# W_in's conversion issued behind P times V of its step instead of ahead of it

## The chip, the cores and the metric

The kernel runs on one core of one Trainium2 chip. The time is that of one execution in device microseconds; a kernel's time is the median of its runs. Engines are called TensorE (PE in the profile, PEld for its weight loads), VectorE (DVE), ScalarE (ACT), GpSimd (POOL) and SyncE (SP, which here only issues DMAs).

## The reference, cut to what matters

```python
scores = q @ k^T / 8                      # 4 batches x 12 heads, 448 x 448, head size 64
p = exp(30 * tanh(scores / 30))           # kept as numerators, divided by their sums later
x = (p / p.sum(-1)) @ v                   # laid out as 1792 x 768
x = soft_moe(x, phi, w1, w2)              # 8 experts, 32 slots in all
out = (prelu(x @ w_in, alpha)) @ w_out    # w_in 768 x 2048, w_out 2048 x 768, both float64
```

The last two weights arrive as float64 (two 32-bit words to a number) and are turned to float32 on the chip.

## The kernel before, in words

**Stages.** Attention takes the 48 heads as 24 pairs. Then come the eight experts (`experts`, weights w1 and w2 streamed from DRAM), and then the network of W_in and W_out (`mlp`).

**The loop around the change.** Attention is one loop over steps g. A pair has four steps, one for each chunk of keys, in the order 0, 3, 1, 2 (chunk 3 holds the tail of 64 keys of both heads). Step g does, in the order of the source: the scores of its chunk and on ScalarE their tanh (line 381) and exp (line 382), both into the tile `p` (`qk`); at a pair's second step the transposes of the next pair's k and q, with a copy `kh` on ScalarE (line 346) and three operations on VectorE (`kl`, `qh`, `ql`); work put off from earlier steps (`run_bg`: row sums, reciprocals, norms, logits, slot sums); loads of k and q two pairs ahead; the store of a W_in piece that was converted two steps before (`store_w_in`, line 680, which also loads the next raw piece, line 660); the conversion of a W_in piece (`conv_w_in`); at some steps a prefetch of expert weights (line 157); and P times V for the chunk of two steps before (`pv`). At steps g = 4i + 1 that chunk is its pair's last: there ScalarE copies the pair's numerators of x from the PSUM tile `o` to `xu` (line 406). `o` has one buffer, so the first P times V of the next pair, one step later, waits for this copy. GpSimd adds the `p` tiles up for the row sums (lines 397, 401, 404).

**The conversion.** W_in has 24 pieces of 128 x 512. Each goes through `to_f32`: one absolute value on ScalarE (line 178), then four operations on VectorE (lines 179, 183, 186, 189), all on the tile `cvbuf`. The steps are 4, 7, 10, 13, 16, 19, 22, 25, 29 and from there every fourth, to 89; 18 of the 24 are thus steps of the `xu` copy. The store of the last piece frees the place of `cvbuf` for expert weights.

**What sets the order.** Each engine runs its instructions in an order fixed at compile time. A planner works through the source order with a clock of its own: an instruction that is not ready by that clock is passed by a later one of its engine that is. `to_f32` ties its absolute value behind the last matmul issued so far (`order[0]`) and its first VectorE operation behind the last `ql` (`latest[0]`); these ties carry no wait on the chip, they only hold the planner. SyncE's queue issues DMAs in its order, and one that waits holds up those behind it.

Of the kernel before, what the change touches and what calls it, by code (L numbers as in the profile page):

```python
# [24 lines left out]
def tile_attention_soft_moe_mlp(ctx, tc, q, k, v, cap, phi, w1, w2, w_in, w_out, alpha, out):  # L25
# [90 lines left out]
    def load_early(after):  # L116

        key = loads[NA]
        where[key] = [load_quarter(*key, c, t, after) for c, t in enumerate(early)]
# [56 lines left out]
    def to_f32(raw, t, after=()):  # L176
        lo, hi = raw[..., 0], raw[..., 1]
        first = nc.scalar.activation(out=t, in_=hi.bitcast(F32), func=AF.Abs, scale=65536.0)
        then = nc.vector.tensor_scalar(out=t, in0=t, scalar1=H_MIN, scalar2=H_MAX, op0=ALU.max, op1=ALU.min)
        for ins, before in zip((first, then), after):  # L180
            tc.add_manual_dep(ins.ins, before.ins.name, NOSYNC, reason="not before its step")
        tu = t.bitcast(U32)
        nc.vector.tensor_scalar(
            out=tu, in0=tu, scalar1=4, scalar2=1, op0=ALU.logical_shift_left, op1=ALU.logical_shift_right
        )
        nc.vector.scalar_tensor_tensor(
            out=tu, in0=lo, scalar=29, in1=tu, op0=ALU.logical_shift_right, op1=ALU.bitwise_or
        )
        nc.vector.scalar_tensor_tensor(
            out=tu, in0=hi, scalar=0x80000000, in1=tu, op0=ALU.bitwise_and, op1=ALU.bitwise_or  # L190
        )
# [35 lines left out]
    def attention():  # L227
        with ExitStack() as pools:
# [69 lines left out]
            def tails(nm, i, src):  # L298
                if nm == "k":
                    for u in range(2):  # L300
                        nc.sync.dma_start(out=ktails[i % 2][head(u), u, :], in_=src[u, KEYS:, :])
                    return
                for u in range(2):
                    nc.sync.dma_start(out=nat["v", i][head(u), 2 * JK, :], in_=src[u, KEYS:, :])

            def load(i, names):
                if i >= NPAIR:
                    return None
                b, m = divmod(i, NP)
                for nm in names:  # L310
                    src = {"k": k, "q": q, "v": v}[nm][b, 2 * m:2 * m + 2]

                    if nm == "q":
                        t = nat_p[i % 2].tile([P, J, 2, D], F32, tag=nm, name=nm)
                        for h in range(2):
                            ins = nc.sync.dma_start(
                                out=t[:, :, h, :], in_=src[h].rearrange("(p j) d -> p j d", j=J)
                            )
                    elif nm == "k":
                        t = nat_p[i % 2].tile([128, 2 * JK, D], F32, tag=nm, name=nm)  # L320
                        by_j = t[:, :2 * JK, :].rearrange("p (j h) d -> p j h d", h=2)
                        for h in range(2):
                            ins = nc.sync.dma_start(
                                out=by_j[:, :, h, :], in_=src[h, :KEYS, :].rearrange("(p j) d -> p j d", j=JK)
                            )
                    else:
                        t = v_p[i % 2].tile([128, 2 * JK + 1, D], F32, tag=nm, name=nm)
                        ins = nc.sync.dma_start(
                            out=t[:, :2 * JK, :].rearrange("p (h j) d -> p h j d", h=2),
                            in_=src[:, :KEYS, :].rearrange("h (p j) d -> p h j d", j=JK),  # L330
                        )
                    nat[nm, i] = t
                    if nm != "q" and (i or nm == "v"):
                        tails(nm, i, src)
                return ins

            def trans_k(i):

                t = nat["k", i].rearrange("p (j h) d -> p j (h d)", h=2)
                ps = aux([128, KEYS + 2 * TAIL], "tr")  # L340
                for j in range(JK):
                    transpose(ps[:, 128 * j:128 * j + 128], t[:, j], ident)
                transpose(ps[:, KEYS:], ktails[i % 2].rearrange("p h d -> p (h d)"), ident)
                kh = stk_p[i % 2].tile([128, KEYS + 2 * TAIL], F32R, tag="kh", name="kh")
                kl = stk_p[i % 2].tile([128, KEYS + 2 * TAIL], F32R, tag="kl", name="kl")
                nc.scalar.activation(out=kh, in_=ps, func=AF.Copy)
                nc.vector.tensor_sub(out=kl, in0=ps, in1=kh)
                stk["k", i] = (kh, kl)
# [17 lines left out]
            def qk(i, c):  # L366

                kh, kl = stk["k", i]
                qh, ql = stk["q", i]
                ps = ps_s.tile([128, 2, 512], F32, tag="s", name="s")  # L370
                for n, (a, b) in enumerate(((kh, qh), (kh, ql), (kl, qh))):
                    flags = dict(start=(n == 0), stop=(n == 2))
                    if c == JK:
                        matmul(ps[:, 0, :S], a[:, KEYS:], b, **flags)
                        continue
                    for u in range(2):
                        o = 128 * c
                        matmul(ps[:, u, :S], a[head(u), o:o + 128], b[head(u)], **flags)
                n = 1 if c == JK else 2
                pe = (ptt_p if c == JK else pt_p).tile([128, n, S], F32, tag="p", name="p")  # L380
                nc.scalar.activation(out=pe, in_=ps[:, :n, :S], func=AF.Tanh)  # L381
                nc.scalar.activation(out=pe, in_=pe, func=AF.Exp, scale=cap_sb)  # L382
                pt[i, c] = pe
# [271 lines left out]
            def load_w_in(i):  # L655
                if i >= ncv:
                    return
                fb, kk = divmod(i, KD)
                craw[i] = cvbuf[:, i % 2].rearrange("p (f t) -> p f t", t=2)
                nc.sync.dma_start(out=craw[i], in_=w_in[kk * 128:(kk + 1) * 128, fb * 512:(fb + 1) * 512, :])  # L660

            ncv = KD * (DFF // 512)
# [6 lines left out]
            def cv_at(n):  # L669
                return cv_steps[n]  # L670

            def conv_w_in(i):
                fb, kk = divmod(i, KD)
                t = cvbuf[:, 2, i % 2 * 512:i % 2 * 512 + 512].bitcast(F32)
                to_f32(craw.pop(i), t, (order[0], latest[0]))
                cout[i] = t
# [8 lines left out]
            def run_bg():  # L685
                while bg and min(bg) <= now[0]:
                    for fn, a in bg.pop(min(bg)):
                        fn(*a)
# [18 lines left out]
            for g in range(NPAIR * J + LAG):  # L707
                now[0] = g
                i, c = divmod(g, J)
                if g == 14:  # L710
                    nc.sync.dma_start(out=alpha_sb, in_=alpha.rearrange("(k p) -> p k", p=128))
                if g == 17:
                    nc.vector.tensor_scalar(out=nalpha_sb, in0=alpha_sb, scalar1=-1.0, scalar2=None, op0=ALU.mult)
                if i < NPAIR:
                    qk(i, CHUNKS[c])
                    if c == 1 and i + 1 < NPAIR:
                        trans_k(i + 1)
                        trans_q(i + 1)
                run_bg()
                if i < NPAIR:  # L720
                    if c == 0:
                        last = load(i + 2, "kq") or last
                    if c == 2:
                        if i == NPAIR - LAG - 1:
                            load_early(last)
                    if g == 2:
                        load_w_in(0)
                        load_w_in(1)
                    for n in range(ncv):
                        if cv_at(n) == g - 2:  # L730
                            store_w_in(n)
                        if cv_at(n) == g:
                            conv_w_in(n)
                    if c == 3 and i in LOADS and may_load() is not None:
                        load_next(last)
                if g >= LAG:
                    n, e = divmod(g - LAG, J)
                    pv(n, CHUNKS[e])
                    if e == J - 1:
                        load(n + 2, "v")  # L740
            order.clear()
            while bg:
                now[0] += 1
# [18 lines left out]
    def tail():  # L762
# [254 lines left out]
        with (  # L1017
# [3 lines left out]
            with tc.tile_pool(name="ex2", bufs=1, reuse_waits="tile", side="right") as ex2_p:  # L1021
# [6 lines left out]
                with (  # L1028
# [9 lines left out]
                    mlp(ps_w, ps_c, ex_p, cv_p, g_p, ob_p, so, cstk)  # L1038

    attention()  # L1040
    tail()

# [29 lines left out]
```

## Time and profile before

| | us |
|---|---|
| median of 3 runs (618.27 to 625.05) | 618.63 |
| profiled execution | 618.59 |
| its span, first to last instruction | 616.20 |
| TensorE busy in the span | 574.9 |
| VectorE busy | 403.6 |
| ScalarE busy | 318.8 |
| GpSimd busy | 162.4 |

The span is one execution; 2.39 us of it lie around the span. Attention fills about the first 276 us, the experts run to about 345 us, the rest is the last network. Busy shares are means over these stages.

### The profile page before, as it was taken

Reading aid. Unit: us, or ns where it says so; the run is one execution under the profiler, and the core shown is the slowest. Engines: PE = TensorE matmul, PEld = TensorE weight load, DVE = VectorE, ACT = ScalarE, POOL = GpSimd, SP = SyncE. Lnnn points to the kernel's source line nnn. Section 1 sums busy time; section 2 is a strip of 40 time slices with the busy share of each in tenths; the row PEclk is TensorE's granted clock in tenths of the full one; section 3 lists DMA queues with packets and bytes.
Section 4 is the critical chain, followed back from the end, with each engine's and each line's share of the span. In section 5 each row is a group of like instructions: output and inputs, shape, how many; then the busy total and the mean of one; then the engine's idle time right before and its main releaser. Section 6 shows DMA issues by size and latency. Waiting matters only on the chain.

```text
span 616.2 us, 10737 instructions
## 1 busy us (share of the span) xinstructions
PE 574.9 (93%) x4110; PEld 386.6 (63%) x4110; DVE 403.6 (65%) x734; ACT 318.8 (52%) x509; POOL 162.4 (26%) x111
## 2 busy tenths in 40 slices
PE   6789889999999999989999899999999999999997
PEld 4344344445444444455455568888888888888886
DVE  4499896697669969551013499999566555555662
ACT  4788788788988778620011366764312121121211
POOL 0667586747574745500000000000000000000000
PEclk9899999999999999988999999999999999999999
DMA  4778877798887781799999999100301010010101
GB/s 104 196 219 214 262 233 242 194 254 234 249 246 212 200 246 48 252 376 373 405 403 406 388 406 391 78 1 1 104 1 51 1 31 22 0 52 2 51 1 51
DMA packets 95169, 110.90 MB, mean 180 GB/s; under 512 B 56208, under 2 KB 70032, under 8 KB 95120
## 3 DMA queue, kind: packets, MB, share of 16 engines
q1 hardware_dynamic: 94976, 110.24, 55.5%
q8 instruction: 32, 0.52, 0.4%
q14 instruction: 17, 0.14, 0.1%
q10 hardware_dynamic: 144, 0.00, 0.0%
HBM read 98.41 MB, written 11.80 MB: 179 GB/s over the span
## 4 chain that ended last, share of the span: by engine, by line
PE 64%; DVE 11%; DMA 10%; ACT 7%; POOL 4%; issue 2%; SPq 1%; ACTq 0%; POOLq 0%
PE oc L946 13%; PE oc L952 13%; PE oc L953 13%; DMA w<-in_moe_w_dram 7%; PE o L279 5%; PE s L279 5%; PE hps L901 2%; ACT p L382 2%; POOL acc L401 2%; PE aps L875 2%; POOL acc L397 2%; ACT p L381 2%; DMA k<-in_k_dram 2%; PE h L815 2%; PE tr L279 1%
## 5 line engine op out<-in xcount | busy, mean ns | idle before, releaser
L952 PE MATMUL oc<-wsp,gh 128*128 128x512 f32 x448 | 151.7, 339 | 0.0
L946 PE MATMUL oc<-wsp,gh 128*128 128x512 f32 x448 | 151.6, 338 | 0.0
L953 PE MATMUL oc<-wsp,gl 128*128 128x512 f32 x448 | 150.7, 337 | 0.0
L917 ACT ACTIVATE gh<-gf 128x256 fp32r<-128x256 f32 (+1 forms) x96 | 43.5, 453 | 132.9 <-DVE gf L916 126.9
L279 PE MATMUL o<-p,v 128*64 128x448 f32 (+1 forms) x384 | 94.0, 568 | 13.1 <-ACT xu L406 13.0
L381 ACT ACTIVATE p<-s 128x896 f32<-128x896 f32 x96 | 78.9, 823 | 29.6 <-PE s L279 18.8
L382 ACT ACTIVATE p<-p,cap 128x896 f32<-128x896 f32 x96 | 91.1, 950 | 2.3
L946 PEld LDWEIGHTS oc<-wsp,gh 128*128 128x128 f32 x448 | 85.0, 190 | 10.7 <-issue 0.9
L953 PEld LDWEIGHTS oc<-wsp,gl 128*128 128x128 f32 x448 | 84.7, 189 | 11.0 <-issue 1.2
L952 PEld LDWEIGHTS oc<-wsp,gh 128*128 128x128 f32 x448 | 85.0, 190 | 9.8 <-issue 0.4
L918 DVE TENSOR_TENSOR gl<-gf,gh 128x256 fp32r<-128x256 f32 (+1 forms) x96 | 45.0, 469 | 45.3 <-ACT gh L917 45.2
L397 POOL TENSOR_TENSOR acc<-p 128x896 f32<-128x896 f32 x24 | 53.6, 2235 | 79.2 <-ACT p L382 79.2
L279 PEld LDWEIGHTS s<-qh,kh 64*128 64x128 f32 (+1 forms) x168 | 17.9, 183 | 66.8 <-issue 27.8
L401 POOL TENSOR_TENSOR acc<-acc,p 64x448 f32<-64x448 f32 x46 | 55.2, 1201 | 3.2
L913 DVE TENSOR_SCALAR mn<-hps,alpha 128x256 f32<-128x256 f32 (+1 forms) x81 | 39.5, 487 | 23.5 <-PE hps L901 23.4
L404 POOL TENSOR_TENSOR acc<-acc,p 128x896 f32<-128x896 f32 x23 | 49.7, 2162 | 1.8
L279 PE MATMUL s<-qh,kh 64*128 64x448 f32 (+1 forms) x168 | 45.3, 469 | 0.0
L279 PEld LDWEIGHTS o<-p,v 128*64 128x64 f32 (+1 forms) x384 | 19.0, 134 | 38.1 <-ACT xu L406 19.3
L916 DVE SCALAR_TENSOR_TENSOR gf<-hps,mn 128x256 f32<-128x256 f32 (+1 forms) x81 | 34.6, 428 | 2.7
L279 PE MATMUL s<-qh,kl 64*128 64x448 f32 (+1 forms) x168 | 35.3, 364 | 0.0
L279 PE MATMUL s<-ql,kh 64*128 64x448 f32 (+1 forms) x168 | 35.1, 363 | 0.0
L837 PE MATMUL y<-w,hT 128*32 128x256 f32 x384 | 30.7, 382 | 1.8 <-DVE hT L830 1.1
(151 smaller groups left out, 780.9 us busy)
## 6 DMA issues: line engine op xcount, KB each, us to landing
w<-in_moe_w_dram SPq DMA_DIRECT2D x80, 384.0 KB, 7.9
w<-in_moe_w_dram SPq DMA_DIRECT2D x36, 512.0 KB, 8.1
cvbuf<-in_moe_w_in_dram SPq DMA_DIRECT2D x24, 512.0 KB, 4.9
w<-in_moe_w_out_dram SPq DMA_DIRECT2D x16, 768.0 KB, 9.0
w_in<-cvbuf SPq DMA_DIRECT2D x24, 256.0 KB, 2.5
q<-in_q_dram SPq DMA_DIRECT2D x48, 112.0 KB, 4.2
k<-in_k_dram SPq DMA_DIRECT2D x48, 96.0 KB, 5.0
v<-in_v_dram SPq DMA_DIRECT2D x24, 192.0 KB, 3.3
```

What stands on the lines that cost most here:

```text
L279: ins = nc.tensor.matmul(*a, **kw)
L381: nc.scalar.activation(out=pe, in_=ps[:, :n, :S], func=AF.Tanh)
L382: nc.scalar.activation(out=pe, in_=pe, func=AF.Exp, scale=cap_sb)
L397: nc.gpsimd.tensor_add(out=a, in0=pt[i, 0], in1=pe)
L401: nc.gpsimd.tensor_add(out=a[r, u, :], in0=a[r, u, :], in1=pt[i, JK][r, 0, :])
L404: nc.gpsimd.tensor_add(out=a, in0=a, in1=pe)
L913: nc.vector.tensor_scalar(out=mn, in0=ps, scalar1=0.0, scalar2=alpha_sb[:, f:f + 1], op0=ALU.min, op1=ALU.mult)
L917: nc.scalar.activation(out=gh, in_=gf, func=AF.Copy)
L918: nc.vector.tensor_sub(out=gl, in0=gf, in1=gh)
L946: ins = nc.tensor.matmul(o, gh[:, ts], wo_h[f][:, cols], start=(f == 0 and not second), stop=False)
L952: nc.tensor.matmul(o, gh[:, ts], wo_l[f][:, cols], start=False, stop=False)
L953: nc.tensor.matmul(o, gl[:, ts], wo_h[f][:, cols], start=False, stop=(f == KF - 1 and not more))
```

## The change

The two lines that issue a step's conversion move from ahead of `pv` to behind it. Everything else in the source stays, and the tie of the absolute value is now to the last matmul of `pv`, since that is the last one issued.

```diff
                     for n in range(ncv):
                         if cv_at(n) == g - 2:
                             store_w_in(n)
-                        if cv_at(n) == g:
-                            conv_w_in(n)
                     if c == 3 and i in LOADS and may_load() is not None:
                         load_next(last)
                 if g >= LAG:
                     n, e = divmod(g - LAG, J)
                     pv(n, CHUNKS[e])
                     if e == J - 1:
                         load(n + 2, "v")
+
+                for n in range(ncv):
+                    if cv_at(n) == g:
+                        conv_w_in(n)
```

## Rows read from the trace of the kernel before

**Rows 1.** Busy time by stretch: us, PE, PEld, DVE, ACT, POOL busy (count), clock, DMA, GB/s.

```profile
20.00:250.00 230.00, 210.52 (x1449) 101.78 (x1449) 184.63 (x277) 192.45 (x265) 150.34 (x89) 0.99 0.76 216
```

**Rows 2.** The chain that ended last, expert stage: start us, us, what.

```profile
299.82 8.67 DMA w<-in_moe_w_dram
...
336.47 7.86 DMA w<-in_moe_w_dram
```

**Rows 3.** Waits of TensorE, 280 to 346 us: total us, times, longest.

```profile
PE y L837 <- DMA w<-in_moe_w_dram: 0.7, 2, 0.4
```

**Rows 4.** Timeline of SyncE's queue, 247 to 252 us: start us, us, instruction.

```profile
248.12 0.33 SPq L680 DMA_DIRECT2D w_in<-cvbuf  x1
250.26 1.76 SPq L157 DMA_DIRECT2D w<-in_moe_w_dram  x4
```

**Rows 5.** Timeline of VectorE, 229 to 249 us.

```profile
231.33 0.42 DVE L179 TENSOR_SCALAR cvbuf<-cvbuf 128x512 f32<-128x512 f32 x1
...
243.52 0.41 DVE L179 TENSOR_SCALAR cvbuf<-cvbuf 128x512 f32<-128x512 f32 x1
...
245.62 2.47 DVE L189 SCALAR_TENSOR_TENSOR cvbuf<-cvbuf 128x512 uint32<-128x512 uint32 x1
```

**Rows 6.** Timeline of ScalarE, 173 to 176 us.

```profile
174.22 0.66 ACT L178 ACTIVATE cvbuf<-cvbuf 128x512 f32<-128x512 f32 x1
174.78 0.53 ACT L406 ACTIVATE xu<-o 128x448 f32<-128x448 f32 x1
```

**Rows 7.** The chain that ended last, five places of attention.

```profile
44.66 0.44 ACT xu L406
...
129.82 0.37 SPq L680
...
155.76 0.56 ACT cvbuf L178
...
156.75 0.82 ACT p L381
...
196.82 0.44 ACT xu L406
```

**Rows 8.** Waits of TensorE, 20 to 250 us: total us, times, longest.

```profile
PE o L279 <- ACT xu L406: 13.0, 12, 3.0
```

**Rows 9.** Timeline of TensorE at three places; in brackets its idle time before.

```profile
45.15 0.97 PE L279 MATMUL o<-p,v 128*64 128x448 f32 x4 [2.01 <-ACT xu L406]
...
172.97 0.97 PE L279 MATMUL o<-p,v 128*64 128x448 f32 x4
...
175.37 0.97 PE L279 MATMUL o<-p,v 128*64 128x448 f32 x4 [0.62 <-ACT xu L406]
...
197.31 0.97 PE L279 MATMUL o<-p,v 128*64 128x448 f32 x4 [0.34 <-ACT xu L406]
```

**Rows 10.** The chain again, at two steps without a copy to `xu`.

```profile
34.64 0.66 ACT cvbuf L178
35.30 0.82 ACT p L381
...
65.19 0.68 ACT cvbuf L178
```

**Rows 11.** Timeline of ScalarE at three of the conversions.

```profile
123.78 0.67 ACT L178 ACTIVATE cvbuf<-cvbuf 128x512 f32<-128x512 f32 x1
...
126.06 0.55 ACT L406 ACTIVATE xu<-o 128x448 f32<-128x448 f32 x1 [0.32 <-PE o L279]
...
230.49 0.68 ACT L178 ACTIVATE cvbuf<-cvbuf 128x512 f32<-128x512 f32 x1
231.91 0.55 ACT L406 ACTIVATE xu<-o 128x448 f32<-128x448 f32 x1 [0.74 <-PE o L279]
...
241.56 0.67 ACT L178 ACTIVATE cvbuf<-cvbuf 128x512 f32<-128x512 f32 x1
```

**Rows 12.** The instructions of line 189: least, median, largest ns; first and last start.

```profile
L189 DVE SCALAR_TENSOR_TENSOR cvbuf<-cvbuf x24: 679/692/2569, 25.3 to 245.6; 128x512 uint32<-128x512 uint32 x24
```

## The prediction

> **What bounds the kernel now.** I read the busy times by stretch first, then the chain that ended last, then who waits for whom around the copy to `xu`, and last the timelines of single engines. In attention no engine alone sets the pace: from 20 to 250 us TensorE is busy for 210.5 of 230 us, ScalarE for 192.5, VectorE for 184.6 [rows 1], and the chain changes engine every few microseconds. What follows attention matters as much. In the expert stage the chain consists of five landings of expert weights in a row, the first 8.67 us long and the last 7.86 us [rows 2]. TensorE nevertheless waits for weights only twice there, for 0.7 us in all [rows 3]. So two paths reach the end of the experts within 0.7 us of each other: TensorE's work, which starts when attention ends, and the stream of weights. Where does the stream start? At 250.26 us, in the place of `cvbuf`, right behind the store of the last W_in piece, which was issued at 248.12 us as soon as the last VectorE operation of the last conversion was through [rows 4, 5]. From there the queue is never without weights to load. Hence the conversion that is moved has two handles on the time: what it does to the steps of attention, and the moment at which its 24th piece is done. A shift of both moves the end by as much; a later stream alone moves it by nearly all of its delay; an earlier attention alone gains nothing, since the stream already comes last.
>
> **What the change does, part by part.** No instruction is added or removed. 24 absolute values on ScalarE move, and with them, in the planner's clock, 96 VectorE operations. They are moved past `pv`: its matmuls on TensorE, the additions that it issues on GpSimd, the copy to `xu` on ScalarE, and on SyncE a load of v. The conversion issues no DMA itself, so SyncE's order stays, and GpSimd's and TensorE's too; on VectorE `pv` has nothing at these steps. What can change is the place of the absolute value on ScalarE, and how long VectorE's queue, with whatever stands in it behind the conversion's first operation, waits for it.
>
> An absolute value takes 0.67 us and holds up the next instruction by 0.56 us (174.22 to 174.78) [rows 6]; the copy to `xu` holds the next one up by 0.44 us [rows 7]. Of the 18 conversions at steps of the copy, 12 stand straight ahead of a copy that then starts without a wait, 5 run in time in which ScalarE would have waited for P times V anyway, and 1 is already behind the copy.
>
> *The wait that is meant.* TensorE waits for the copy 12 times, for 13.0 us in all [rows 8]. In eight of these places the absolute value stands ahead of the copy; the first of them waits 2.01 us, the last 0.34 us, and the eight make 6.2 us [rows 9]. The copy can come forward by 0.56 us at most, and TensorE gains no more than its wait: four places with over 0.56 us give 0.56 each, the other four 0.20, 0.20, 0.23 and 0.34, together 3.2 us. The place at 175.37 us is a clean one: P times V is through at 173.94 us (172.97 and 0.97), so the copy can take the absolute value's start at 174.22 us, and the wait of 0.62 us falls to 0.06 us [rows 6, 9]. What is late next there is TensorE itself.
>
> *How much of it counts.* Only where the chain runs through the copy into P times V does TensorE's gain carry on. That is so at four of the eight places, the first at 44.66 us and the last at 196.82 us [rows 7]; their gains are 0.56, 0.20, 0.56 and 0.34, so 1.66 us. At two others the chain stays on ScalarE, from the absolute value through the copy to the next tanh at 156.75 us [rows 7]: whichever goes first, both are ahead of that tanh. There the copy may in addition have to wait for P times V, which the absolute value does not; that costs between 0 and 0.56 us each, and I take the middle, 0.56 us for both. The last two hang on VectorE and on a load, and I count them at nothing.
>
> *The other steps.* At two of the steps without a copy the absolute value even runs ahead of its own step's tanh, at 34.64 and at 65.19 us, and both times the chain goes through it [rows 10]. Tied to the matmuls of P times V, which come behind those of the scores, it should fall behind that tanh: twice 0.56, so 1.12 us gained. The remaining steps I take at nothing: there it stands between a tanh and its exp, and whether it stays there is open.
>
> *What is lost.* At the five places where ScalarE waits before the copy, the absolute value is free now. At 230.49 us it runs while ScalarE has nothing else; the copy comes at 231.91 us after an idle wait of 0.74 us. At 123.78 us it is the same, with 0.32 us of waiting left [rows 11]. Behind the copy it would start at 231.91 + 0.44 = 232.35 us and end at 233.0 us, and the conversion's first VectorE operation, now at 231.33 us [rows 5], would come 1.7 us later. VectorE's queue is in order, so what stands behind that operation waits too, unless the planner lets other work pass. The price is between 0 and 1.7 us; I take half, 0.85 us, because VectorE has some work that does not need the piece. At 123.78 us the same delay reaches the store, which waits for the conversion, and the k load behind it in SyncE's queue; the chain does pass through that store at 129.82 us [rows 7]. I take 0.85 us there as well, with the same ends. The other three of the five are not on the chain.
>
> *The last piece.* Its absolute value runs from 241.56 us for 0.67 us, with the copy behind it [rows 11]; in the changed order it would end 0.44 us later, at 242.7 us, and VectorE takes up the piece only at 243.52 us [rows 5]. So 0.8 us of cover is left and the stream's start shifts only with the rest of attention.
>
> *Sum.* Gained 1.66 + 1.12 = 2.78 us, lost 0.56 + 0.85 + 0.85 = 2.26 us: 0.5 us less. The profiled execution took 618.59 us, the median is 618.63 us, so there is nothing to correct between them. **Forecast: 618.1 us**, no change that can be told.
>
> **A rule that speaks against the change.** The conversion's last operation takes 0.69 us in the median and 2.57 us at worst [rows 12]; the last piece's takes 2.47 us [rows 5]. The Trainium skill, page "SBUF — State Buffer", section "Who interferes with whom", says that a VectorE instruction with two SBUF inputs and a GpSimd instruction that reads SBUF exclude each other, and whichever comes second is blocked until the first is through. The long instances agree with that. By this rule a conversion that is done later, in an attention step in which GpSimd's additions start soon after, gets one more of its operations caught; that is the third rival's second part.
>
> **The rivals.**
>
> 1. *The order on ScalarE stays.* The planner fills gaps: at 34.64 us it put the absolute value ahead of a tanh of its own step although the tanh stands first in the source and both hang on the same matmuls [rows 10]. The tie is thus satisfied when the matmul is placed, while the copy needs it finished. Where the planner sees ScalarE idle at that point, the absolute value again goes first. Against it: on the chip P times V is through before ScalarE is free at several of the places, as at 173.94 us, and there the copy should win. Time: 618.6 us.
>
> 2. *All of the gain and none of the loss.* Every place of the eight gives its share, 3.2 us, with the 1.12 us of the other steps, and the idle time at the five places is filled in another way: 618.6 - 4.3 = 614.3 us. For it speaks that TensorE is the busiest engine; against it, that only four of the eight places are on the chain.
>
> 3. *Slower: the weight stream starts later.* The place is VectorE from the 23rd to the 24th piece. If the 23rd piece's first operation waits its full 1.7 us and nothing passes it, what VectorE has to do before 248 us is late by that much, and with it the store and the stream: 620.3 us. If moreover one more operation of the last piece is caught behind a GpSimd addition, 2.57 - 0.69 = 1.9 us come on top: 622.2 us. It decides when the absolute value of the last piece ends later than 243.5 us, or the 23rd piece's first operation keeps VectorE idle. For it: the stream's start is tied to this piece alone [rows 4]. Against it: the slack of 0.8 us, and work that can pass.
>
> **How the numbers follow.** The forecast, gains and losses mixed and between 616.5 and 619.5 us, gets 0.52; the unchanged order, which falls in the same stretch, 0.17; the full gain 0.12; the later stream 0.19. The range reaches from the full gain, 614.3 us, to the later stream with the caught operation, 622.2 us. A measurement of this kernel can tell about 2%, 12.4 us, from no change. No case comes near it: it is nearly all of the 13.0 us that TensorE waits for the copy. I leave 0.02 for faster and 0.03 for slower, for an order of the planner that none of the cases has, and 0.95 for the same.
>
> **What would show it.** In the changed profile the copy to `xu` should start 0.2 to 0.56 us behind the exp's issue with no absolute value between, TensorE's wait for the copy should fall from 13.0 us to about 10 us, and ScalarE should wait longer for P times V. The absolute values at the third and seventh piece should stand behind a tanh. VectorE should wait for the absolute value, which it now hardly does. The store of the last piece, now at 248.12 us, should come between 246 and 250 us, and the end should move with it. I would be wrong if the copy's place is unchanged, if the store moves and the end does not, or if the end moves by more than 4 us either way.

## The result, and the profile after

The changed kernel takes 621.95 us in the median of 11 runs, the kernel before 619.14 us beside it: ratio 1.0062, 95% interval 1.0036 to 1.0088, so 3.8 us slower (2.2 to 5.4). (The two medians alone, divided, give 1.0045, or 2.8 us; from here on the ratio with its interval is used.) The time lies in the range; the sign of the forecast, 0.5 us less, is wrong. The profiled execution took 622.31 us, with a span of 619.9 us.

The two stages first: attention by windows (columns as in [rows 1]), and TensorE's wait for the copy, which stands beside [rows 8].

```profile
20.00:250.00 230.00, 209.25 (x1432) 100.40 (x1432) 185.81 (x273) 190.81 (x262) 148.25 (x88) 0.99 0.76 215
```

```profile
PE o L279 <- ACT xu L406: 12.4, 12, 3.1
```

In 230 us attention got through 17 matmuls and 3 ScalarE instructions less than before, and the wait that the change is meant for fell from 13.0 to 12.4 us only, still 12 times. Why so little, ScalarE's timeline says: at the clean place of the prediction [rows 6, 9].

```profile
176.45 0.67 ACT L178 ACTIVATE cvbuf<-cvbuf 128x512 f32<-128x512 f32 x1
177.01 0.54 ACT L406 ACTIVATE xu<-o 128x448 f32<-128x448 f32 x1
```

The absolute value is still ahead of the copy. Instruction for instruction, ScalarE's order differs at eight of the 24 conversions (steps 7, 10, 13, 19, 22, 45, 69 and 89), and at only two of the 18 steps of the copy (13 and 89) does the copy newly go first. Of the steps without a copy four changed, among them 10 and 22, as forecast; the absolute value of step 22 is behind the tanh now, where it was ahead [rows 10]:

```profile
64.28 0.92 ACT L381 ACTIVATE p<-s 128x896 f32<-128x896 f32 x1
65.09 0.67 ACT L178 ACTIVATE cvbuf<-cvbuf 128x512 f32<-128x512 f32 x1
```

Something else changed where nothing good was expected of it. At step 45 (before: [rows 11], 123.78 and 126.06) both the absolute value and the copy come later: the planner put the exponential of the softmax over tokens, L566, between them.

```profile
126.38 0.66 ACT L178 ACTIVATE cvbuf<-cvbuf 128x512 f32<-128x512 f32 x1
126.94 0.62 ACT L566 ACTIVATE ls<-lr,nm_run 128x448 f32<-128x448 f32 x1
...
127.55 0.54 ACT L406 ACTIVATE xu<-o 128x448 f32<-128x448 f32 x1
```

VectorE there, first in the kernel before, then in the changed one. `dl` holds the exponentials of the softmax over tokens and the logits, laid out the other way; `c_all` is the softmax over slots that is made from it.

```profile
128.07 0.69 DVE L189 SCALAR_TENSOR_TENSOR cvbuf<-cvbuf 128x512 uint32<-128x512 uint32 x1
...
129.40 0.41 DVE L606 COPY dl<-nd 112x256 f32<-112x256 f32 x1
...
130.53 0.91 DVE L645 TENSOR_TENSOR c_all<-dl,mx 112x128 f32<-112x128 f32 x1
```

```profile
127.07 0.43 DVE L179 TENSOR_SCALAR cvbuf<-cvbuf 128x512 f32<-128x512 f32 x1 [0.68 <-ACT cvbuf L178]
...
130.02 0.68 DVE L189 SCALAR_TENSOR_TENSOR cvbuf<-cvbuf 128x512 uint32<-128x512 uint32 x1
130.62 0.42 DVE L606 COPY dl<-nd 112x256 f32<-112x256 f32 x1
...
131.56 1.24 DVE L645 TENSOR_TENSOR c_all<-dl,mx 112x128 f32<-112x128 f32 x1
```

The conversion's first operation waits 0.68 us, its last (L189) has been passed by other work and now stands straight ahead of `dl`, and `c_all` follows 1.0 us later than before. ScalarE waits for `c_all`, 0.27 us before and 0.82 us now, and TensorE for the next copy, 0.20 us before and 0.71 us now:

```profile
131.47 0.31 ACT L646 ACTIVATE c_all<-c_all 112x128 f32<-112x128 f32 x1 [0.27 <-DVE c_all L645]
```

```profile
132.84 0.31 ACT L646 ACTIVATE c_all<-c_all 112x128 f32<-112x128 f32 x1 [0.82 <-DVE c_all L645]
...
137.74 0.97 PE L279 MATMUL o<-p,v 128*64 128x448 f32 x4 [0.71 <-ACT xu L406]
```

Two steps on, the delay grows. On VectorE `rh` (line 463) and the L189 of a later piece, whose place on ScalarE is the old one, now fall beside GpSimd's additions and take longer. A copy to `xnat` that stands between the two is late with them, and TensorE waits 0.65 us for it, where it did not wait before. First the kernel before, then the changed one:

```profile
142.14 1.22 DVE L463 SCALAR_TENSOR_TENSOR rh<-rh,masks,sums 128x224 fp32r<-128x224 f32 x1
...
147.94 0.68 DVE L189 SCALAR_TENSOR_TENSOR cvbuf<-cvbuf 128x512 uint32<-128x512 uint32 x1
```

```profile
144.34 2.25 DVE L463 SCALAR_TENSOR_TENSOR rh<-rh,masks,sums 128x224 fp32r<-128x224 f32 x1
...
150.41 1.98 DVE L189 SCALAR_TENSOR_TENSOR cvbuf<-cvbuf 128x512 uint32<-128x512 uint32 x1
...
150.55 0.42 PE L279 MATMUL ss<-xnat,dl 112*32 112x128 f32 x8 [0.65 <-DVE xnat L502]
```

ScalarE's tanh, 1.3 us behind the kernel before at 149.65 us, is 2.2 us behind it at 153.88 us.

At the end of attention, the last piece on VectorE and the store in SyncE's queue, beside [rows 4, 5]:

```profile
246.22 0.41 DVE L179 TENSOR_SCALAR cvbuf<-cvbuf 128x512 f32<-128x512 f32 x1
...
247.60 2.48 DVE L186 SCALAR_TENSOR_TENSOR cvbuf<-cvbuf 128x512 uint32<-128x512 uint32 x1
250.11 1.51 DVE L189 SCALAR_TENSOR_TENSOR cvbuf<-cvbuf 128x512 uint32<-128x512 uint32 x1
```

```profile
251.65 0.33 SPq L680 DMA_DIRECT2D w_in<-cvbuf  x1
253.80 1.76 SPq L157 DMA_DIRECT2D w<-in_moe_w_dram  x4
```

The store comes 3.53 us later (248.12 before), the first weights 3.54 us (250.26), the end of the span 3.7 us. So nearly all of the loss is there when the stream starts, and next to nothing behind it adds to it. From its first operation (L179) to its store the last piece takes 5.43 us, where it took 4.60 (243.52 to 248.12): VectorE's copy to `xnat` now goes ahead of L183 (246.55 and 247.15 us), and two operations take long where it was one. So of the 3.5 us by which the stream is late 2.7 come with attention, and 0.8 are made at the last piece.

### The profile page after: what moved, and what is told of

It is laid out like the page before. It is cut to its first block, busy times and chain, and to the rows that moved or that the text cites. A ratio compares the mean times of both kernels' runs of the same rounds, so it can differ in the third digit from the quotient of the medians.

```text
span 619.9 us, 10735 instructions
## 1 busy us (share of the span) xinstructions
PE 577.0 (93%) x4110; PEld 387.4 (62%) x4110; DVE 407.6 (66%) x734; ACT 318.9 (51%) x509; POOL 162.2 (26%) x111
## 4 chain that ended last, share of the span: by engine, by line
PE 57%; DMA 17%; DVE 11%; ACT 6%; SPq 3%; POOL 2%; issue 2%; ACTq 0%; POOLq 0%
PE oc L948 13%; PE oc L954 13%; PE oc L955 13%; DMA w<-in_moe_w_dram 11%; PE o L279 4%; DMA k<-in_k_dram 4%; PE s L279 3%; PE hps L903 2%; ACT p L382 2%; PE aps L877 2%; DVE cvbuf L189 2%; DVE cvbuf L186 2%; ACT p L381 2%; DVE cvbuf L183 1%; DMA q<-in_q_dram 1%
## 5 line engine op out<-in xcount | busy, mean ns | idle before, releaser
L279 PE MATMUL o<-p,v 128*64 128x448 f32 (+1 forms) x384 | 94.8, 572 | 12.6 <-ACT xu L406 12.4
L948 PEld LDWEIGHTS oc<-wsp,gh 128*128 128x128 f32 x448 | 85.0, 190 | 10.7 <-issue 0.9
```

The source lines that it names most:

```text
L279: ins = nc.tensor.matmul(*a, **kw)
L948: ins = nc.tensor.matmul(o, gh[:, ts], wo_h[f][:, cols], start=(f == 0 and not second), stop=False)
```

## The experiments

Each kernel below was timed in five rounds against the kernel before on its chip; percentages and the microseconds worked out from them (times 618) are from these ratios, with the 95% interval behind. Single waits come from one profiled execution each.

**Which conversions cost.** Three kernels with the move for some pieces only. Pieces are numbered 0 to 23; 12 is at step 45, 18 at 69, 22 at 85, 23 at 89.

```diff
-                        if cv_at(n) == g:
+                        if cv_at(n) == g and n not in BEHIND:
                             conv_w_in(n)
...
+                for n in range(ncv):
+                    if cv_at(n) == g and n in BEHIND:
+                        conv_w_in(n)
```

BEHIND = 0 to 7:

> Only the pieces of steps 4 to 25 (the first eight) are converted behind P times V; the others stay ahead of it. Theory: the loss is made at steps 45, 69, 85 and 89, where work of the softmax over the tokens or the last store hangs on the conversion, and the early steps give and take the same; then 0 us, between -0.8 and +0.8 us, unless TensorE's half-clock stretch near 25 us is longer than before, which adds about 0.9 us by itself. Rival: the early steps, in which the absolute value moves between a tanh and its exp and VectorE waits for it up to 1.3 us at a time, make most of the loss: +2 to +3 us.

BEHIND = 22, 23:

> Only the last two pieces (steps 85 and 89) are converted behind P times V. Theory: the last piece's VectorE operations come some 0.5 to 1.2 us later, the store of the piece and the stream of expert weights start that much later, and the end moves by the same: +0.5 to +1.2 us, with the store's issue near 248.9 us in place of 248.12 us. Rival: the end does not hang on the store, since TensorE works without a wait until 343 us: 0 us, with the store later and the end where it was.

BEHIND = 12, 18:

> Only the pieces of steps 45 and 69 are converted behind P times V; there the planner puts the absolute value and the exp of the softmax over tokens ahead of the copy to xu. Theory: each of the two places costs 0.5 to 0.9 us, because the copy, the next tanh and the VectorE work behind the conversion come later, and it lasts: +1.0 to +1.8 us. Rival: the places have slack, and what is lost is caught up within a pair: 0 us, between -0.4 and +0.4 us.

Measured: the early pieces +0.12% (-0.13 to 0.36), the late two +0.20% (-0.04 to 0.44), pieces 12 and 18 alone +0.38% (0.23 to 0.54), which is 2.3 us (1.4 to 3.3). The three add up to 0.70%, the whole change is 0.62%. The two conversions beside the softmax over tokens make the largest share, and the only one told from nothing. For the early pieces the rival's 2 us lie just inside the interval.

**The move as it was meant.** All 24 pieces behind P times V, and at the 18 steps of the copy the absolute value tied to the copy itself, in the planner alone, so that the copy really goes first (`copied[0]` is the last copy to `xu`; the kernels with this tie have a line more, so that copy is L407 there).

```diff
-                to_f32(craw.pop(i), t, (order[0], latest[0]))
+                to_f32(craw.pop(i), t, (copied[0] if i in FORCED else order[0], latest[0]))
```

> All pieces are converted behind P times V, and at the 18 steps with a copy to xu the absolute value is tied behind the copy itself, so that the copy really is first everywhere. Theory (the planner's gap filling took the gain away): TensorE's wait for the copy falls from 13.0 to about 9 us and the time is 1 to 2.5 us below that of the changed kernel, near the kernel before. Rival (what counts is the conversion's lateness, not the copy): the wait falls as well, but VectorE gets its piece later at all 18 places, and the time is the changed kernel's or 1 to 3 us above it.

Measured: +1.38% (1.16 to 1.60), 8.5 us, so 4.7 us above the changed kernel: the theory fails, and even the rival named less. TensorE's waits for the copy did not fall:

```profile
PE o L280 <- ACT xu L407: 14.4, 10, 3.1
```

They are two fewer than before, but two new long ones, 2.3 us each, stand right behind steps 45 and 69. At 111 us, where no such step has come yet, this kernel's TensorE was 1.0 us ahead of the kernel before (at its transposes; at the next P times V it was 0.6). That is not told from the spread of single executions: the kernels in which the first twelve pieces stay where they were stand between 0.2 us behind and 0.7 us ahead at the same place. The two long waits ask for the two halves apart.

**The halves.** The first kernel moves 14 of the 18 (FORCED = BEHIND = 3, 7 to 11, 13 to 17, 19 to 21) and leaves everything else as before; the second moves only 12, 18 and 22.

> 14 of the 18 conversions at steps of the copy go behind P times V and really behind the copy to xu; those at the softmax over tokens (steps 45, 69), step 85 and the last (89) stay ahead, as before. Theory: the loss arises only at the steps left out, where the conversion's VectorE work, once late, falls in front of dl and c_all, on which ScalarE waits. Then this kernel keeps the gain that the fully forced one showed up to 111 us, 1.0 us, and a little at later places: 616.0 to 617.6 us against 618.1. Rival: every late conversion delays its store, and the k load behind the store in SyncE's queue; then 14 of them cost 1 to 3 us: 619 to 621 us.

> Only the conversions of steps 45, 69 and 85 go behind P times V and behind the copy to xu. Theory: these three carry most of the 8.5 us that the fully forced kernel lost: 622 to 626 us, with ScalarE waiting over 2 us for VectorE's c_all near 133 us and TensorE over 2 us for xu right after. Rival (the loss is spread over all 18 steps): 618.5 to 620 us.

Measured: the 14 take 0.32% off (0.21 to 0.43), 2.0 us, and make the fastest version of this study that leaves nothing out, 617.02 us in the median beside 618.87. The three alone cost 2.04% (1.63 to 2.45), 12.6 us, more than the fully forced kernel lost and more than the 4 to 8 us expected. Both signs of the theory, the two waits of over 2 us, hold. In the kernel of the 14, TensorE's wait for the copy, and the ScalarE waits that grew; beside them ScalarE's in the kernel before:

```profile
PE o L280 <- ACT xu L407: 10.6, 9, 2.6
...
ACT p L382 <- POOL acc L398: 6.1, 11, 0.9
ACT p L382 <- POOL acc L402: 5.4, 10, 0.8
```

```profile
ACT p L381 <- POOL acc L401: 5.4, 9, 1.1
...
ACT p L381 <- POOL acc L397: 2.4, 6, 0.8
```

The copy's wait falls by 2.4 us. ScalarE's tanh, which needs a `p` tile that GpSimd's additions have let go of, waits 11.5 us for them in place of 7.8, and 12.6 us for TensorE's scores in place of 16.4: what is late next there is GpSimd rather than TensorE. The gain is made late. In the traced execution the copy to `xu` of step 45 is 0.7 us later than in the kernel before, that of step 81 is 0.6 us earlier; the lead at 111 us, on which the expectation was built, is not there.

In the kernel of the three, around step 45: VectorE, GpSimd, ScalarE and TensorE.

```profile
129.88 2.48 DVE L189 SCALAR_TENSOR_TENSOR cvbuf<-cvbuf 128x512 uint32<-128x512 uint32 x1
132.28 0.41 DVE L607 COPY dl<-nd 112x256 f32<-112x256 f32 x1
```

```profile
129.31 2.51 POOL L398 TENSOR_TENSOR acc<-p 128x896 f32<-128x896 f32 x1 [5.91 <-ACT p L383]
```

```profile
133.55 0.31 ACT L647 ACTIVATE c_all<-c_all 112x128 f32<-112x128 f32 x1 [2.44 <-DVE c_all L646]
```

```profile
138.25 1.61 PE L280 MATMUL o<-p,v 128*64 128x448 f32 x4 [2.47 <-ACT xu L407]
```

L189 starts 0.57 us behind GpSimd's addition and lasts 2.48 us, to 132.36; the addition ends at 131.82. In the kernel before, L189 was through (128.76 us) when that addition began. From there it is one line: `dl` 2.9 us later than before, ScalarE without work for 2.44 us, TensorE without work for 2.47 us. In the changed kernel the same L189 began at 130.02 us and the addition at 130.05 us, and it took 0.68 us: it went through by 0.03 us.

```profile
130.05 2.60 POOL L397 TENSOR_TENSOR acc<-p 128x896 f32<-128x896 f32 x1 [5.84 <-ACT p L382]
```

This time the addition took the delay, 2.60 us where it took 2.11 us before. That is the rule which the prediction named (the Trainium skill, "SBUF — State Buffer", "Who interferes with whom"): whichever comes second is blocked. The rows agree on both sides. Over the whole kernel of the three, the median of L189 is 1.52 us, against 0.69 [rows 12].

```profile
L189 DVE SCALAR_TENSOR_TENSOR cvbuf<-cvbuf x24: 681/1518/2582, 26.4 to 255.0; 128x512 uint32<-128x512 uint32 x24
```

**The store and the k load.** The prediction had put the price of step 45 on SyncE's queue. The kernel of the three again, with their stores (and the raw loads that go with them) two steps later:

```diff
-                        if cv_at(n) == g - 2:
+                        if cv_at(n) == g - (4 if n in BEHIND else 2):
```

> As the kernel before it in this call (steps 45, 69 and 85 behind the copy), but the stores of these three pieces, and the raw loads tied to them, are issued two steps later, so that no k load stands behind a store that waits for the late conversion. Theory (VectorE's queue: dl and c_all behind the late conversion): as slow as that kernel, within 1 us. Rival (SyncE's queue: the k load behind the waiting store): back to 618 to 619 us.

Measured: +1.71% (1.42 to 1.99), 10.6 us; the interval overlaps that of the kernel of the three and is far from the rival's 618 to 619 us. The k load of that step now goes out at 129.29 us in place of 133.25 us, and ScalarE waits as long as before:

```profile
129.29 1.26 SPq L324 DMA_DIRECT2D k<-in_k_dram  x2
```

```profile
133.55 0.31 ACT L647 ACTIVATE c_all<-c_all 112x128 f32<-112x128 f32 x1 [2.42 <-DVE c_all L646]
...
138.25 1.02 PE L280 MATMUL o<-p,v 128*64 128x448 f32 x2 [2.48 <-ACT xu L407]
```

So in this kernel the queue is not the cause of these waits: the load came 4 us earlier and neither wait moved. For the changed kernel itself no such run was made.

**The last piece alone** (BEHIND = 23, no tie).

> Only the last conversion (step 89) goes behind P times V. Theory of the prediction's last piece (0.8 us of cover): 618.1 us, 0.5 us either way, the last store within 0.5 us of 248.1 us. Rival (the stream of weights starts later by what the changed kernel showed, 3.5 us): 620 to 622 us.

Measured: +0.07% (-0.05 to 0.20), and the last store at 248.42 us against 248.12.

```profile
243.00 0.41 DVE L179 TENSOR_SCALAR cvbuf<-cvbuf 128x512 f32<-128x512 f32 x1
```

```profile
248.42 0.33 SPq L681 DMA_DIRECT2D w_in<-cvbuf  x1
```

The later stream of the changed kernel is thus for the most part not made at the last piece; it comes with attention. But the store's small shift hides something: in this execution L179 came 0.52 us earlier than before, and from it to the store it took 5.42 us, the time of the changed kernel, in place of 4.60. By the trace the last piece costs 0.8 us; the runs (0.4 us, -0.3 to 1.2) do not tell that from nothing.

**Where the price lies within a conversion.** Two ways to take the late VectorE work out of the softmax's way. In the first, the last two operations of the three conversions are issued behind the softmax's last operation, three steps later (`conv_rest`, tied to the last `c_all` in the planner; stores two steps later, as above); nothing is left out. In the second, they are left out, with a control.

```diff
+                    if cv_at(n) == g - 3 and n in BEHIND:
+                        conv_rest(n)
```

> As the kernel with the three pieces of steps 45, 69 and 85 behind the copy and their stores two steps later, with one difference: the last two VectorE operations of these three conversions are issued behind the softmax's last c_all, three steps later, so that dl and c_all go ahead of them. ScalarE's order stays the late one; nothing is left out. Theory (VectorE's last operations, late and caught behind GpSimd's additions, hold up dl and c_all): the loss of about 10.6 us against before nearly vanishes, 617.5 to 620 us. Rival (ScalarE's order, xu and the exponential of the softmax ahead of the absolute value, or the place of the store): stays at 626 us or more.

> Steps 45, 69 and 85 behind the copy, stores where they were; the last two VectorE operations of these three conversions are left out, so their pieces are not converted to the end. Theory: without them nothing long stands ahead of dl and c_all: 616.5 to 619.5 us, at most 1.5 us from its control. Rival (the late absolute value and the wait of VectorE's first operation for it already cost): over 5 us above its control.

> Control: the kernel before, with the same six VectorE operations left out. Both theories: 616.5 to 618.5 us, since VectorE's work there is not on the path as long as it comes early.

Measured: left out, +0.08% (-0.17 to 0.34) and the control -0.23% (-0.44 to -0.03); so what is left without the two operations (ScalarE's changed order, the wait for the absolute value, the first two operations late) costs about 0.31%, 1.9 us, with an interval from about nothing to 0.6% (an estimate from the two ratios). That is a little more than the 1.5 us expected, and some 10.7 of the 12.6 us hang on the two late VectorE operations. ScalarE's wait for `c_all` is 0.47 us without them, against 0.26 us in the control.

For the changed kernel this says something else. There pieces 12 and 18 cost 2.3 us, about as much as is left here without the two operations, and there L189 went through in 0.68 us at both steps. The trace of this kernel also has what follows two steps on in the changed kernel: the second operation on `rh` takes 2.25 us, a later piece's last operation 1.98 us, and TensorE waits 0.65 us for `xnat`; its control has none of the three (1.22 us, 0.68 us, no wait). So the two late operations, caught at their own step, are what the tie to the copy adds. Which of the three things that are left makes the price of the change as it was written was not taken apart.

Issued later, the loss grew to +2.85% (2.44 to 3.25), where next to none was expected. Its first half came as the theory says: `dl` and `c_all` go first, and ScalarE's wait falls from 2.44 to 0.48 us.

```profile
129.28 0.42 DVE L618 COPY dl<-nd 112x256 f32<-112x256 f32 x1
```

```profile
131.84 0.31 ACT L658 ACTIVATE c_all<-c_all 112x128 f32<-112x128 f32 x1 [0.48 <-DVE c_all L657]
```

But the two operations only moved on to the next work. In VectorE's timeline L199 (L189 of the kernel before) is caught, `qh` to `ql` of the next pair come late (from 137.26 us), and then all four operations of the next piece run into GpSimd's additions:

```profile
135.28 2.06 DVE L199 SCALAR_TENSOR_TENSOR cvbuf<-cvbuf 128x512 uint32<-128x512 uint32 x1
...
139.05 1.98 DVE L181 TENSOR_SCALAR cvbuf<-cvbuf 128x512 f32<-128x512 f32 x1
141.06 1.25 DVE L185 TENSOR_SCALAR cvbuf<-cvbuf 128x512 uint32<-128x512 uint32 x1
142.34 1.52 DVE L194 SCALAR_TENSOR_TENSOR cvbuf<-cvbuf 128x512 uint32<-128x512 uint32 x1
143.89 2.44 DVE L199 SCALAR_TENSOR_TENSOR cvbuf<-cvbuf 128x512 uint32<-128x512 uint32 x1
```

```profile
146.73 0.90 PE L291 MATMUL tr<-ident,k 128*128 128x128 f32 x3 [3.46 <-DVE s_run L648]
```

The four take 7.2 us instead of the 2.2 us of their short form, and TensorE waits 3.46 us for a copy behind them. The theory needs a wider wording: not `c_all` as such is what the late work harms, but whatever stands behind it in VectorE's queue.

**The change without its bad places.** As written, no tie, BEHIND = all but 12, 18, 22, 23.

> The change as it was written, for all pieces but those of steps 45, 69, 85 and 89, with no tie to the copy. Theory: the planner keeps its old order at most of these steps, so neither gain nor loss: 617.5 to 619 us, against 616.9 us where the copy really goes first. Rival (the gain needs only the move): 616 to 617.3 us.

Measured: -0.06% (-0.28 to 0.16). The move alone buys nothing measurable at these 20 pieces; with the tie, 14 of them give 0.32%. The two intervals just overlap.

## Why the prediction failed

**Two steps failed.** The forecast missed by 4.3 us, 0.5 us less against 3.8 us more. The larger share is the gain: "The wait that is meant" and "How much of it counts" let the copy take the absolute value's start, which gave 1.66 us, and "The other steps" gave 1.12 us; no run shows any of these 2.78 us for the change as it was written. The other 1.5 us are losses, 3.8 us measured against 2.26 us in the sum. Without the gain the same losses would have given the right sign.

**What is lost** was read too low. Of the five places where ScalarE waits before the copy it priced 230.49 and 123.78 us, 0.85 us each, and let the others go: "The other three of the five are not on the chain." One of those three is step 69, and it behaves like step 45: in the kernel of the three pieces TensorE waits 2.47 us behind one and 2.44 us behind the other, and in the changed kernel ScalarE's wait for `c_all` there grows from 0.44 to 0.73 us. Both are steps of the softmax over tokens. The absolute value ran there in ScalarE's idle time, and so its four VectorE operations were through before GpSimd's additions began and before `dl` came. The chain of before could not show this, because nothing was late. Pieces 12 and 18 together cost 2.3 us (1.4 to 3.3), where the sum had 0.85 us.

**The mechanism at 123.78 us** was also another, as far as the runs show. The prediction put it on the store and the k load behind it. That store is on the chain of the changed kernel too, but taking the k load out from behind it in the kernel of the three pieces moved neither wait.

**The gain** of 1.66 us from the copy going first did not come, since the absolute value stayed ahead of the copy at 15 of the 18 steps. That is the order of the first rival, which I gave 0.17, though not its time: the tie to a matmul is satisfied when the matmul is placed, the copy needs it finished, and the planner put the absolute value into the gap. "On the chip P times V is through before ScalarE is free" was no argument, for the planner decides by its own clock. With the copy forced ahead at 14 steps, 2.0 us (1.3 to 2.7) were gained, so the size was about right, but by another path than place by place: the wait at the clean place is 0.74 us there against the 0.06 us forecast. The copy stands right behind the exp, as forecast, but ScalarE itself has fallen back: its tanh, which waits for GpSimd, starts 0.45 us behind that step's P times V (173.77 and 173.32 us), where it started 0.23 us ahead of it.

**The 1.12 us** at steps 10 and 22 were right as to order, and yet the first eight pieces together measured +0.12% (-0.13 to 0.36). A larger wait between them shows how easily such a gain moves on. In the kernel before the copy of step 21 waited 2.06 us until VectorE's `xn` had let go of its buffer, and `xn` stood behind a caught L189 (61.65 us, 2.48 us long):

```profile
64.75 0.55 ACT L406 ACTIVATE xu<-o 128x448 f32<-128x448 f32 x1 [2.06 <-DVE xn L487]
```

In the changed kernel this wait is gone, and the copy of the next pair has it:

```profile
75.11 0.54 ACT L406 ACTIVATE xu<-o 128x448 f32<-128x448 f32 x1 [2.05 <-DVE xn L487]
```

This does not explain the missing gain by itself: in the kernel of the first eight pieces neither copy waits for `xn`, and it is not faster either.

**The piece at 230.49 us** was priced at 0.85 us. The two late pieces measure 1.2 us (-0.2 to 2.7), the last alone 0.4 us (-0.3 to 1.2): it fits, but is not told from nothing.

**The last piece** was half right. Its absolute value has its cover, L179 follows `ql` without a wait; but behind it VectorE's order changed, one more operation was caught, and that cost 0.8 us in the traces. The rest of the late stream comes with attention. The third rival, slower through a later stream by way of the last two pieces, named the right sign and a fitting time, 620.3 to 622.2 us, and even the caught operation; but it put the whole at the end of attention, and the larger part was made at steps 45 and 69. That the time fell into the range is thus in part luck.

What stays open: what exactly makes the price of steps 45 and 69 in the change as it was written. The kernel of the three pieces lost 12.6 us by its runs and about 8 us in its profiled execution, whose time is at the fast end of them; in which places the other runs lost more, no trace shows. That GpSimd's additions stretch the VectorE operations rests on their times side by side; a kernel in which only the additions are moved wasn't tried.

## What to carry to other kernels

Work that runs in an engine's idle time costs nothing where it stands; before moving it, read what stands behind its followers on the next engine's in-order queue, even if the chain does not pass there. A planner-only tie to an operation that is merely placed does not force an order: tie to the operation that is to go first, and check the order of the engine. And a move that helps at most steps may be ruined by few: here 14 conversions moved behind the copy gained 2.0 us and three others cost 12.6.

## What the hardware showed

TensorE's clock fell behind the long waits. In the kernel of the three pieces TensorE stood idle for 2.47 us, having been busy before, and ran the next 3.5 us at a granted clock of 0.53, so nearly at the lower of its two levels, 1.2 of 2.4 GHz: P times V took 1.61 us in place of 0.97. By windows, columns as in [rows 1]:

```profile
135.50:138.20 2.70, 0.27 (x4) 0.00 (x0) 2.70 (x4) 2.70 (x7) 1.24 (x1) 1.00 0.71 197
138.20:141.70 3.50, 3.45 (x22) 1.49 (x26) 3.40 (x6) 2.16 (x3) 1.55 (x1) 0.53 0.65 148
```

The same follows its wait of 2.44 us near 203 us, and the 3.46 us in the kernel with the later operations (0.50). The mean granted clock is 0.977 in the kernel of the three and 0.989 in the kernel before. These waits are thus paid twice, as idle time and in the slower matmuls behind. Not every wait is: behind its 2.25 us at 65.35 us the kernel before ran the next 3.65 us at 1.00.

The time of a blocked operation is not small change: operations of 0.41 to 0.69 us took 1.25 to 2.58 us beside GpSimd, among them L181 and L185, which have one tensor input (lines 179 and 183 of the kernel before), so two inputs are not a condition for it.
